# Four second-layer weight tiles loaded and prepared between the last expert's two units

## The chip, the core and the metric

The kernel runs on one core of one Trainium2 chip. The metric is the device time of one execution in microseconds (us). The core has a matrix engine (PE, with its weight loads shown apart as PEld), a vector engine (DVE), a scalar engine (ACT), GpSimd (POOL), and a queue (SP) that issues most of the transfers between the chip's memory and on-chip buffers. Each engine works through its own list of instructions in order and waits for the others by semaphores.

## What is computed

Three layers follow each other: attention, a mixture of eight experts in which each token goes to one, and a dense layer with a gate. Cut to what matters here:

```
def _moe_ref(x, w_gate, w_output_gate, w1, w2):      # x: 1536 x 512
    ...
    for e in range(E):                               # 8 experts
        mask = e_idx == e
        h = np.maximum(x[mask] @ w1[e], 0.0)         # 512 -> 1024
        ye = h @ w2[e]                               # 1024 -> 512
        out[mask] = gate_w[mask, None] * eom[mask, e, None] * ye

def _moe2_ref(x, w_in, w_out):                       # w_in: 512 x 2048
    h = x @ w_in
    g = h * (1.0 / (1.0 + np.exp(-h)))
    return (g @ w_out).astype(np.float32)            # w_out: 2048 x 512
```

The weights of the dense layer come as 64-bit floats.

## The kernel before

Each float32 matrix product is made of three matmuls: operands are split into a rounded high part and the rest as a low part, and high x high, high x low and low x high are summed.

**Experts.** `moe1` (L1042) runs ten units one after the other. A unit is some rows of one expert: two tiles of 128 rows, or one. The last two, here called unit A and unit B, are the first and the second 128 rows of expert 0. In `expert` (L965) such a one-tile unit first makes 2 x 12 matmuls `hr` (L986) in two groups. ACT copies each group to a buffer named `stage` (L989), PE transposes it (`htp`, L992), and `split` (L898) turns it into a high part (ACT, L899) and a low part (DVE, L904), both called `H`. Then 24 matmuls `yp` (L1022) make the output, DVE scales it into `ys` (L1027), and POOL scatters its rows to the table `x2` in memory (L824). Between unit A's two halves, the rows of unit B are transposed (`etp`) and split into `X`. Unit A's rows all belong to the first 768 tokens, so that the first block of the dense layer waits for unit A's scatter and not for unit B's.

**Dense layer.** `moe2` (L1218) has three blocks of 512 tokens. `load2` (L1204) reads a block's rows from `x2` (L834), transposes them (`tp`, L1213) and splits them into `XH` and `XL`; for the first block this stands in the middle of unit B. A block has 16 steps f. A step makes 12 matmuls `hp` (L1259), a sigmoid on ACT (L1265), a product on DVE (`sg`, L1266), a split into `GH` (ACT) and `GL` (DVE), and 12 matmuls `op` (L1238), which PE does one step late or more.

**Preparing a tile.** The dense layer has 16 weight tiles: four of `w_in` for f 0 to 7, four of `w_out` for f 0 to 7, and the same again for f 8 to 15, listed in that order by `weights2` (L1157). A tile is prepared in two halves of 512 columns. For each, SP loads 512 KB into a `stage` buffer (L1170); ACT scales the upper words (L1178) and copies the top bytes (L1181); DVE masks (L1182) and shifts (L1183) to put a 32-bit float together; ACT writes the high part of `w` (L899) and POOL the low part (L904):

```
nc.scalar.activation(gf, gf, AF.Copy, scale=float(2.0 ** (-112)))
nc.scalar.activation(l, by, AF.Copy, scale=1.0 / 32, bias=-31.0 / 64)
nc.vector.scalar_tensor_tensor(l, g, 2147483648, l, op0=ALU.bitwise_and, op1=ALU.bitwise_or)
nc.vector.scalar_tensor_tensor(g, g, 3, l, op0=ALU.logical_shift_left, op1=ALU.bitwise_or)
s.split(hi[:, sl], lo[:, sl], gf, s.nc.gpsimd)
```

There are seven `stage` buffers during the experts and four in the dense layer, used in turn; the one-tile units take one of the seven each for `hr`.

**Who orders the work.** The list `seq` in `moe1` holds the loads that are still to be made: 60 tiles of experts and then the 16 of the dense layer. Every unit takes up to four from it in its first half and up to four in its second, except those of expert 0, which take what the list `ta` says. Before, `ta` holds zeros: the eight earlier units take 60 expert tiles and 4 dense ones, and the 12 that are left are prepared in the first block of the dense layer, one at each of its steps f 0 to 11 (`w2.pop(0)()`). Inside a stage the order on each engine is fixed when the program is built.

Of the kernel before, what the change touches and what calls it, by code (L numbers as in the profile page):

```python
# [634 lines left out]
class Moe:  # L635
# [406 lines left out]
    def moe1(s, w2, free):  # L1042
        tc = s.tc
        nc = s.nc
        pos = 6
        L = 0
        N1 = 12
        N0 = 8
        units = [(e, 0, 2) for e in range(1, pos)] + [(E, 0, 1)] + [(e, 0, 2) for e in range(pos, E)] + [(L, 0, 1), (L, 1, 1)]
        order = [u[0] for u in units[:-1]]  # L1050
        W = {}
        X = {}
        s.ew = {e: s.expert_weights(e) for e in range(E)}

        def item(e, i):
            if e == E and i == 0:
                with tc.issue_after(s.lastld):
                    ev = nc.sync.value_load(s.Ei[0:1, 0:1], min_val=0, max_val=E - 1)
                s.ew[E] = s.expert_weights(ev)
            W.setdefault(e, [None] * 8)[i] = s.ew[e][i]()  # L1060

        def prep(u):
            e, h, n = u
            xt = s.rows('xt', s.xo, slice(0, 128), 1) if e == E else s.rows('xt', s.xst, slice(e * CAP + h * 128, e * CAP + (h + n) * 128), n, apart=u == units[0])
            x = s.lift(xt, n)
            X[u] = (s.labels(xt, n), x)
        s.hold = s.hold0
        for i in range(N0):
            if i == 4:
                s.hold = 2  # L1070
                with tc.issue_after(s.lastlow):
                    for _ in s.plan2:
                        pass
                s.lastlow = s.lastplan
            item(order[0], i)
        s.hold = False

        idle = s.ps_h.tile([128, 512], F32, tag='h', name='idle')
        with tc.issue_after(s.att.lastpe):
            for _ in range(33):  # L1080
                r = nc.tensor.matmul(idle, lhsT=s.ones, rhs=s.tri.unsqueeze(1).to_broadcast([128, 4, 128]), start=True, stop=True)
        with tc.issue_after(r.ins):
            prep(units[0])
        with tc.issue_after(s.lastlow):
            for f in s.lows:
                f()
        with tc.issue_after(s.lastrow), tc.issue_after(s.lastlow):
            for i in range(N0, 8):
                item(order[0], i)
            for i in range(N1 - 8):  # L1090
                item(order[1], i)
        s.gp = free()
        seq = [lambda e=e, i=i: item(e, i) for e in order for i in range(8)][N1:] + w2
        take = lambda n: [seq.pop(0) for _ in range(min(n, len(seq)))]
        x2 = []
        ta = [0, 0, 0, 0]
        for p, u in enumerate(units):
            e, h, n = u
            fx, x = X.pop(u)
            def first2():  # L1100
                x2.append(s.load2(0))

                idle = s.ps_h.tile([128, 512], F32, tag='h', name='idle2')
                with tc.issue_after(s.lasttp):
                    for _ in range(10):
                        nc.tensor.matmul(idle, lhsT=s.ones, rhs=s.tri.unsqueeze(1).to_broadcast([128, 4, 128]), start=True, stop=True)
            nxt = (lambda: prep(units[p + 1])) if p + 1 < len(units) else first2
            a, b = (4 if p else 16 - N1, 4) if e != L else ta[2 * h:2 * h + 2]
            s.expert(fx, x, n, W[e], take(a), nxt, take(b), first=p == 0)
        sig = s.fp.tile([128, 2, 4], F32, tag='f', name='sig')  # L1110
        with tc.high_priority(), tc.issue_after(s.lasth):
            nc.scalar.activation(sig[:, 0, 0:1], s.ident[:, 0:1], AF.Sigmoid)
        return (x2[0], seq)
# [218 lines left out]
```

## Time and profile before

| | us |
|---|---|
| median of three timed runs | 778.09 (777.33 to 779.23) |
| the profiled execution | 782.32 |
| its span, from the first to the last instruction | 780.2 |
| PE busy | 738.0 (95% of the span) |
| DVE busy | 485.6 (62%) |
| ACT busy | 436.6 (56%) |
| POOL busy | 322.7 (41%) |
| unit A's first matmul | at 456.5 |
| first block of the dense layer, first matmul | at 488.3 |

All places in time below are microseconds from the start of the span of the profiled execution. PE's busy time is that of pipelined matmuls whose ends overlap the next one's start: how many of them start in a stretch tells more of its pace than the busy share does. Busy time of the other engines counts an instruction from its start to its end, with what it waits for inside.

### The profile page before, as it was taken

How to read it: one execution, taken by the hardware profiler on the slowest of the kernel's cores; microseconds unless marked ns; L12 is line 12 of the kernel's file. 1: busy time of each engine (PE TensorE's matmuls, PEld its weight loads, DVE VectorE, ACT ScalarE, POOL GpSimd, SP SyncE). 2: the span in 40 equal slices, each digit the busy share in tenths (PEclk: the TensorE clock that was granted, in tenths of full speed). 3: DMA queues.
4: the chain of work that ended last, by engine and by line, in shares of the span. 5: the costliest groups of instructions: out<-in, count | busy, mean ns of one | idle time of the engine just before them, and what ended most of it. 6: DMA issues, size and time to landing. Idle time of an engine off the chain costs nothing.

```text
span 780.2 us, 14156 instructions
## 1 busy us (share of the span) xinstructions
PE 738.0 (95%) x5540; PEld 626.2 (80%) x5540; DVE 485.6 (62%) x823; ACT 436.6 (56%) x711; POOL 322.7 (41%) x259
## 2 busy tenths in 40 slices
PE   7889999999998799999999999989999999999995
PEld 6678998999998398888978877766787888878884
DVE  5769788877977666896568952899624222232222
ACT  5768889889875346655456653878423122131212
POOL 4677887878653376653334360455300000000000
PEclk9789999999999999999999999999999999999998
DMA  8769899998994578976557714666101000010001
GB/s 272 163 140 234 182 180 163 209 182 159 219 184 167 181 251 312 316 259 241 207 190 274 223 54 172 218 189 210 43 1 55 0 1 1 0 55 1 0 1 57
DMA packets 132984, 116.31 MB, mean 149 GB/s; under 512 B 97607, under 2 KB 103751, under 8 KB 132912
## 3 DMA queue, kind: packets, MB, share of 16 engines
q1 hardware_dynamic: 129632, 109.03, 52.3%
q0 software_dynamic: 3280, 6.33, 2.2%
q8 instruction: 45, 0.74, 0.4%
q14 instruction: 27, 0.22, 0.1%
HBM read 71.67 MB, written 18.45 MB: 116 GB/s over the span
## 4 chain that ended last, share of the span: by engine, by line
PE 61%; DVE 18%; issue 7%; ACT 6%; DMA 5%; POOL 2%; DVEq 0%; SPq 0%; ACTq 0%; POOLq 0%
PE op L1238 14%; PE hp L1259 13%; PE yp L1022 8%; PE hp L1006 6%; DVE m L423 4%; PE sp L402 3%; DMA stage<-in_moe_w_in 2%; PE sp L404 2%; PE hr L986 2%; DVE pt L460 2%; PE tp L190 2%; PE ptp L449 2%; ACT w L899 2%; PE cl L207 1%; POOL w L904 1%
## 5 line engine op out<-in xcount | busy, mean ns | idle before, releaser
L904 POOL TENSOR_TENSOR w<-stage,w 128x512 fp32r<-128x512 f32 (+1 forms) x54 | 105.1, 1953 | 98.8 <-ACT w L899 81.8
L1259 PE MATMUL hp<-XH,w 128*128 128x512 f32 (+1 forms) x392 | 124.0, 394 | 3.7 <-DVE sg L1266 3.5
L1238 PE MATMUL op<-w,GH 128*128 128x512 f32 x384 | 113.5, 396 | 0.1
L423 DVE TENSOR_REDUCE m<-sp 128x1 f32<-128x768 f32 x96 | 91.2, 951 | 34.4 <-PE sp L404 31.0
L469 POOL TENSOR_TENSOR p<-p,p 128x768 f16<-128x768 f32 x58 | 95.2, 1649 | 34.0 <-DVE p L468 18.5
L899 ACT ACTIVATE w<-stage 128x1024 fp32r<-128x1024 f32 (+1 forms) x104 | 94.7, 939 | 20.5 <-DVE stage L1183 8.2
L1266 DVE TENSOR_TENSOR sg<-hp,sg 128x512 f32<-128x512 f32 (+1 forms) x49 | 33.2, 678 | 111.8 <-ACT sg L1265 111.8
L425 ACT ACTIVATE p<-sp,m 128x768 f32<-128x768 f32 x96 | 86.1, 897 | 14.1 <-DVE m L423 13.9
L904 DVE TENSOR_TENSOR w<-stage,w 128x1024 fp32r<-128x1024 f32 x50 | 86.9, 1759 | 8.6 <-ACT w L899 8.5
L1265 ACT ACTIVATE sg<-hp 128x512 f32<-128x512 f32 (+1 forms) x49 | 28.8, 587 | 113.4 <-PE hp L1259 112.3
L1259 PEld LDWEIGHTS hp<-XH,w 128*128 128x128 f32 x392 | 73.2, 188 | 22.9 <-DVE sg L1266 5.4
L1006 PEld LDWEIGHTS hp<-X,w 128*128 128x128 f32 x672 | 84.8, 190 | 8.5 <-DVE HL L1008 4.0
L1006 PE MATMUL hp<-X,w 128*128 128x256 f32 x672 | 87.7, 284 | 4.1 <-DVE HL L1008 2.2
L1238 PEld LDWEIGHTS op<-w,GH 128*128 128x128 f32 x384 | 71.9, 188 | 17.7 <-ACT GH L899 1.0
L1259 PE MATMUL hp<-XL,w 128*128 128x512 f32 (+1 forms) x196 | 75.1, 391 | 0.0
L1238 PE MATMUL op<-w,GL 128*128 128x512 f32 x192 | 69.0, 399 | 3.5 <-DVE GL L904 3.3
L1022 PE MATMUL yp<-w,HH 128*128 128x512 f32 x224 | 68.9, 397 | 0.0
L402 PE MATMUL sp<-KA,QA 128*128 128x384 f32 x192 | 62.5, 407 | 2.9 <-ACT p L425 2.3
L493 PE MATMUL o<-vh,pt 128*128 128x66 f16 x576 | 62.0, 195 | 0.4 <-DVE pt L460 0.4
L494 PE MATMUL o<-vl,pt 128*128 128x64 f16 x576 | 61.5, 192 | 0.0
L495 PE MATMUL o<-vh,pt 128*128 128x66 f16 x576 | 61.1, 192 | 0.0
L493 PEld LDWEIGHTS <-pt 128*128 128x128 f16 x576 | 52.3, 96 | 7.2 <-issue 5.9
(221 smaller groups left out, 1454.7 us busy)
## 6 DMA issues: line engine op xcount, KB each, us to landing
stage<-in_moe_w SPq DMA_DIRECT2D x72, 512.0 KB, 4.8
stage<-in_moe_w_in SPq DMA_DIRECT2D x16, 512.0 KB, 4.3
stage<-in_moe_w_out SPq DMA_DIRECT2D x16, 512.0 KB, 4.5
xst<-z SPq DMA_DIRECT2D x8, 516.0 KB, 5.4
xt<-xst SPq DMA_DIRECT2D x6, 516.0 KB, 5.1
vt<-in_v SPq DMA_DIRECT2D x4, 768.0 KB, 6.6
xt<-x SPq DMA_DIRECT2D x6, 512.0 KB, 4.3
out_x<-os SPq DMA_DIRECT2D x12, 256.0 KB, 2.5
```

The source lines that it names most:

```text
L402: nc.tensor.matmul(sp[:, g, :384], lhsT=QA[:, t], rhs=KAf[:, g * 384:(g + 1) * 384], start=True, stop=False)
L423: st['min'] = nc.vector.tensor_reduce(m, sv, axis=AX.XY, op=ALU.min).ins
L425: st['exp'] = nc.scalar.activation(p32, sv, AF.Exp, bias=m, scale=-1.0).ins
L469: s.nc.gpsimd.tensor_sub(p16[:, 1], p32, p16[:, 0])
L493: nc.tensor.matmul(o[:, t, 0:D + 2], lhsT=pt[:, 0, kt], rhs=vh[:, kt], start=kt == 0, stop=False)
L494: nc.tensor.matmul(o[:, t, 0:D], lhsT=pt[:, 0, kt], rhs=vl[:, kt], start=False, stop=False)
L899: s.lasthi = s.nc.scalar.activation(hi, src, AF.Copy).ins
L904: f = lambda: (eng or s.nc.vector).tensor_sub(lo, src, hi).ins
L1006: nc.tensor.matmul(hp, lhsT=W1[k][w][:, f * 128:(f + 1) * 128], rhs=x[:, k, :N], start=n == 0, stop=n == 11)
L1022: nc.tensor.matmul(yp, lhsT=h[:, f, i * 128:(i + 1) * 128], rhs=w, start=n == 0, stop=n == 23)
L1238: nc.tensor.matmul(op[i], lhsT=g[:, i * 128:(i + 1) * 128], rhs=w, start=f == 0 and m == 0, stop=f == 15 and m == 2)
L1259: nc.tensor.matmul(h, lhsT=I[k, f // 8][w][:, fs], rhs=x[:, k, c], start=n == 0, stop=n == 11)
```

## The change

Two entries of the list become 2. Unit A therefore takes two dense-layer tiles from the list in its first half and two in its second: the four of `w_out` for f 0 to 7. The eight tiles that are left are prepared at the steps f 0 to 7 of the first block.

```diff
@@ -1093,7 +1093,7 @@
         seq = [lambda e=e, i=i: item(e, i) for e in order for i in range(8)][N1:] + w2
         take = lambda n: [seq.pop(0) for _ in range(min(n, len(seq)))]
         x2 = []
-        ta = [0, 0, 0, 0]
+        ta = [2, 2, 0, 0]
         for p, u in enumerate(units):
```

What this does to the engines' lists, at three places. The numbers behind names count buffers; the halves of the four tiles are `stage_7185`, `7193`, `7202`, `7210`, `7279`, `7287`, `7296` and `7304` in the changed kernel.

POOL, from the scatters of the unit ahead of unit A to that of unit B. The scatter of unit A is the one of `ys_7244` before and `ys_7312` now, that of unit B the next one. Before:

```order
L904 TENSOR_TENSOR w_7139<-stage_7148,w_7139 128x512
L824 DMA x2_72<-ys_7092,f_6733 1536x512
L824 DMA x2_72<-ys_7156,f_6733 1536x512
L824 DMA x2_72<-ys_7244,f_6969 1536x512
L824 DMA x2_72<-ys_7363,f_7215 1536x512
```

and now:

```order
L824 DMA x2_72<-ys_7092,f_6733 1536x512
L824 DMA x2_72<-ys_7156,f_6733 1536x512
L904 TENSOR_TENSOR w_7184<-stage_7185,w_7184 128x512
L904 TENSOR_TENSOR w_7184<-stage_7193,w_7184 128x512
L904 TENSOR_TENSOR w_7201<-stage_7202,w_7201 128x512
L904 TENSOR_TENSOR w_7201<-stage_7210,w_7201 128x512
L824 DMA x2_72<-ys_7312,f_6969 1536x512
L904 TENSOR_TENSOR w_7278<-stage_7279,w_7278 128x512
L904 TENSOR_TENSOR w_7278<-stage_7287,w_7278 128x512
L904 TENSOR_TENSOR w_7295<-stage_7296,w_7295 128x512
L904 TENSOR_TENSOR w_7295<-stage_7304,w_7295 128x512
L824 DMA x2_72<-ys_7431,f_7249 1536x512
```

Four subtractions now stand ahead of unit A's scatter, and four more ahead of unit B's.

ACT, from the split of unit B's rows (`X`) to the split of its hidden rows (`H`). Before:

```order
L899 ACTIVATE X_7207<-etp_7208 128x4x128
L989 ACTIVATE stage_7249<-hr_7251 128x512
L989 ACTIVATE stage_7249<-hr_7272 128x512
L899 ACTIVATE H_7250<-htp_7265 128x512
L899 ACTIVATE H_7250<-htp_7286 128x512
```

and now the end of the same piece, from the scaling of the seventh half:

```order
L1178 ACTIVATE stage_7296<-stage_7296 128x512
L1181 ACTIVATE stage_7296<-stage_7296 128x512
L899 ACTIVATE w_7278<-stage_7279 128x512
L1178 ACTIVATE stage_7304<-stage_7304 128x512
L1181 ACTIVATE stage_7304<-stage_7304 128x512
L899 ACTIVATE w_7278<-stage_7287 128x512
L989 ACTIVATE stage_7317<-hr_7319 128x512
L899 ACTIVATE w_7295<-stage_7296 128x512
L989 ACTIVATE stage_7317<-hr_7340 128x512
L899 ACTIVATE w_7295<-stage_7304 128x512
L899 ACTIVATE H_7318<-htp_7333 128x512
L899 ACTIVATE H_7318<-htp_7354 128x512
```

Unit B's two `H` copies now stand behind the high part of the eighth half, which waits for DVE's shift of it. In unit A, likewise, the scaling and byte copy of the second half now stand between the copy of `hr` and the two `H` copies; DVE's mask of that half stands ahead of its first `H`, and its masks and shifts of the last four halves stand ahead of unit B's `H`. On SP the eight loads stand ahead of the two reads of the first block's rows (`xt`), where none stood.

DVE, in the first block of the dense layer, from the step f 7 on. Before, to f 8:

```order
L1266 TENSOR_TENSOR sg_7725<-hp2_7724,sg_7725 128x512
L1182 SCALAR_TENSOR_TENSOR stage_7893<-stage_7893 128x512
L1183 SCALAR_TENSOR_TENSOR stage_7893<-stage_7893 128x512
L904 TENSOR_TENSOR GL_7727<-sg_7725,GH_7726 128x512
L1182 SCALAR_TENSOR_TENSOR stage_7934<-stage_7934 128x512
L1183 SCALAR_TENSOR_TENSOR stage_7934<-stage_7934 128x512
L1182 SCALAR_TENSOR_TENSOR stage_7942<-stage_7942 128x512
L1183 SCALAR_TENSOR_TENSOR stage_7942<-stage_7942 128x512
L1266 TENSOR_TENSOR sg_7774<-hp2_7773,sg_7774 128x512
```

and now, to f 9:

```order
L1266 TENSOR_TENSOR sg_7793<-hp2_7792,sg_7793 128x512
L904 TENSOR_TENSOR GL_7795<-sg_7793,GH_7794 128x512
L1266 TENSOR_TENSOR sg_7842<-hp2_7841,sg_7842 128x512
L904 TENSOR_TENSOR GL_7844<-sg_7842,GH_7843 128x512
L1266 TENSOR_TENSOR sg_7908<-hp2_7907,sg_7908 128x512
```

The masks and shifts that stood here are gone; the last of the eight tiles' shifts now stands ahead of f 6.

## Rows read from the trace of the kernel before

**Rows 1.** Stretches: length, then busy us (instructions) of PE, PEld, DVE, ACT, POOL, granted clock, DMA share, GB/s.

```profile
456.00:488.00 32.00, 31.39 (x151) 23.91 (x149) 11.30 (x16) 12.91 (x24) 11.87 (x10) 1.00 0.33 125
488.30:510.00 21.70, 21.69 (x97) 17.64 (x98) 18.43 (x24) 16.94 (x31) 10.46 (x7) 1.00 0.67 208
510.00:534.00 24.00, 20.46 (x87) 15.24 (x87) 23.03 (x25) 19.19 (x34) 13.27 (x10) 1.00 0.62 186
534.00:558.00 24.00, 21.68 (x89) 15.21 (x89) 22.21 (x25) 18.46 (x32) 13.67 (x9) 1.00 0.47 152
```

**Rows 2.** Waits of PE from 380 on: total us, times, longest.

```profile
PE hp L1259 <- DVE sg L1266: 3.5, 5, 1.4
PE op L1238 <- DVE GL L904: 3.3, 4, 1.6
```

**Rows 3.** The chain that ended last, a step behind the first block's preparation: start, us.

```profile
571.91 2.80 PE hp L1259 x12
```

**Rows 4.** Groups by line, 534 to 558: count, busy us, mean ns, idle before.

```profile
L1213 PE MATMUL tp<-ident,xt 128*128 128x128 f32 x8 | 1.2, 272 | 0.0
```

**Rows 5.** Order of time, DVE: start, us; the shift of the eighth tile's second half.

```profile
531.49 1.71 DVE L1183 SCALAR_TENSOR_TENSOR stage<-stage 128x512 uint32<-128x512 uint32 x1
```

**Rows 6.** Order of time, DVE's shift and POOL's subtraction, beside each other and alone.

```profile
455.85 1.32 POOL L904 TENSOR_TENSOR w<-stage,w 128x512 fp32r<-128x512 f32 x1 [3.93 <-issue]
455.96 1.76 DVE L1183 SCALAR_TENSOR_TENSOR stage<-stage 128x512 uint32<-128x512 uint32 x1
...
457.13 1.77 POOL L904 TENSOR_TENSOR w<-stage,w 128x512 fp32r<-128x512 f32 x1
...
499.87 0.69 DVE L1183 SCALAR_TENSOR_TENSOR stage<-stage 128x512 uint32<-128x512 uint32 x1
```

**Rows 7.** Groups by line, DVE, 488 to 558.

```profile
L1183 DVE SCALAR_TENSOR_TENSOR stage<-stage 128x512 uint32<-128x512 uint32 x24 | 31.4, 1312 | 0.6
```

**Rows 8.** Order of time, POOL, around unit A.

```profile
455.85 8.11 POOL L904 TENSOR_TENSOR w<-stage,w 128x512 fp32r<-128x512 f32 x6 [3.93 <-issue]
464.12 0.99 POOL L824 DMA_INDIRECT x<-ys,f  x1 [0.16 <-issue]
...
472.40 0.97 POOL L824 DMA_INDIRECT x<-ys,f  x1 [6.00 <-DVE ys L1027]
```

**Rows 9.** Order of time, SP: the dense layer's loads and the reads behind them.

```profile
430.10 20.47 SPq L1170 DMA_DIRECT2D stage<-in_moe_w_in  x8
475.09 0.89 SPq L834 DMA_DIRECT2D xt<-x  x2
```

**Rows 10.** Issues at 450.2 and at 475.1: KB, us from issue to landing.

```profile
stage<-in_moe_w_in SPq DMA_DIRECT2D x1, 512.0 KB, 3.6
...
xt<-x SPq DMA_DIRECT2D x1, 512.0 KB, 3.7
```

**Rows 11.** Order of time, ACT, in units A and B.

```profile
463.68 0.60 ACT L989 ACTIVATE stage<-hr 128x512 f32<-128x512 f32 x1 [3.55 <-PE hr L986]
464.17 0.59 ACT L899 ACTIVATE H<-htp 128x512 fp32r<-128x512 f32 x1
...
477.47 0.59 ACT L899 ACTIVATE H<-htp 128x512 fp32r<-128x512 f32 x1
```

**Rows 12.** Order of time, DVE, in units A and B.

```profile
471.37 0.75 DVE L1027 TENSOR_SCALAR ys<-yp,f 128x512 f32<-128x512 f32 x1 [3.81 <-PE yp L1022]
478.09 0.69 DVE L904 TENSOR_TENSOR H<-htp,H 128x512 fp32r<-128x512 f32 x1 [5.97 <-ACT H L899]
```

**Rows 13.** Order of time, PE, in units A and B.

```profile
465.95 5.38 PE L1022 MATMUL yp<-w,H 128*128 128x512 f32 x22
...
478.94 0.63 PE L1213 MATMUL tp<-ident,xt 128*128 128x128 f32 x4
```

**Rows 14.** PE at the experts' start: a wait, then two stretches (columns of rows 1).

```profile
271.46 0.66 PE L961 MATMUL etp<-ident,xt 128*128 128x128 f32 x4 [2.51 <-DMA xt<-xst]
...
269.60:273.00 3.40, 1.31 (x8) 0.84 (x8) 3.40 (x13) 0.63 (x2) 0.00 (x0) 1.00 0.97 276
273.10:276.50 3.40, 2.88 (x13) 2.88 (x14) 2.80 (x13) 0.67 (x2) 1.97 (x2) 0.50 0.98 335
```

## Prediction

> **What bounds the kernel now.** I read the stretches first, then PE's waits, then the engines' lists in order of time around units A and B. In the experts' last two units, 456 to 488, PE is busy 31.4 of 32.0 us while DVE, ACT and POOL stand idle for more than half of it [rows 1]. A reader should see two things there: the other engines have room, and PE has none, so that whatever makes PE wait here is paid in full. In the first block of the dense layer it is the other way round: from 510 to 558 DVE is busy 45.2 of 48.0 us and PE waits, for `sg` 3.5 us and for `GL` 3.3 us in all, nearly all of it here [rows 1, 2].
>
> The loss there is larger than those waits, so I take it from counts. Undisturbed, twelve matmuls start in 2.80 us, 0.233 us each [rows 3]. From 534 to 558 PE starts 89, eight of them transposes that take 1.2 us [rows 1, 4]: 81 x 0.233 + 1.2 = 20.1, so 3.9 of the 24 us are lost. From 510 to 534 it starts 87; with as many transposes, 79 x 0.233 + 1.2 = 19.6, 4.4 lost. From 488 to 510, with 97 instructions in 21.7 us, nothing is lost. The first block thus pays about 8.3 us for preparing twelve tiles.
>
> **What the change gives back.** The eighth tile's last shift ends at 533.2 [rows 5]. The four tiles that leave the block are those behind it, so what is lost from 534 on goes: **3.9 us**. Its lower end is 3.2, if the transposes are priced as matmuls (24 - 89 x 0.233), or if the eighth tile's last steps still hold PE for a moment; its upper end is 4.4, half of the loss plus the like of the first stretch. The eight earlier tiles keep their place against the block's steps, so their 4.4 us stay. What is removed from the block (8 loads, 16 ACT steps and 8 copies, 16 DVE steps, 8 on POOL) is added to units A and B; nothing disappears.
>
> **What it costs, first stop: unit A.** I call the eight halves h1 to h8. Each needs one of seven buffers, freed by POOL's subtractions of the tiles before: six in 8.11 us from 455.85, 1.35 each [rows 8], so that h1 to h6 can be issued from 457.2 to 464.0, one behind the other. A load lands after 3.6 us [rows 10]: h1 at 460.8, h2 at 462.5, h3 at 463.6. They are in time. But ACT now scales h2 and copies its bytes between the copy of `hr` that ends at 464.28 and the first `H`, which began at 464.17 [rows 11]: two steps of about 0.6 us. `H` starts at 465.4, DVE's mask of h2 comes next, then `H`'s low part, and the 22 `yp` that began at 465.95 [rows 13] begin at about 467.4. This is **1.4 us**, all on PE. It hides behind nothing, since PE's list has no other work there.
>
> **Second stop: unit B, by the port.** The shift took 1.76 us while POOL's subtraction ran from 455.85 to 457.17, and 0.69 alone; the next subtraction, behind that shift, took 1.77 instead of 1.3 [rows 6]. Over the block the shifts average 1.31 [rows 7]. So a mask or shift and a subtraction exclude each other, and when both wait they take turns. Each half then needs about 0.6 (mask) + 0.6 (shift) + 1.3 (subtraction) = 2.5 us of one resource, as long as the subtractions follow closely. Eight halves are 20 us; the first mask can start at 462.2, behind h1's two ACT steps. I followed the lists from there with these durations. DVE: shift of h2 ends at 467.3, of h3 at 469.7, of h4 at 472.1, of h5 at 474.4 (behind h3's subtraction), `ys` of unit A at 475.1 (before: 472.1 [rows 12]), shift of h6 at 476.9, of h7 at 479.3 (behind h5's subtraction), mask of h8 at 481.1, shift of h8 at 482.9. ACT's high part of h8 ends at 483.6, and only then come unit B's `H` (before 477.47 [rows 11]), their low parts, and the transposes of the first block. h8's buffer is that of h1, free at 468.5; it lands at 472, so its load holds nobody.
>
> The low part of the first `H` ends at 484.85, where it ended at 478.78 [rows 12]; the transposes `tp` that began at 478.94 [rows 13] begin at 484.9. That is **5.9 us** for both stops together, the 1.4 contained. The later blocks' reads and the block's own first loads shift with it and are waited for no longer than before.
>
> **Third path, POOL's scatter and SP.** Unit A's scatter stood alone at 472.40; the read of its rows was issued at 475.09, 2.69 later, and landed after 3.7 us, at 478.8 [rows 8, 9, 10], which is just when the transposes began. So this path has no slack. Now four subtractions stand ahead of the scatter; the fourth, h4's, whose high part leaves ACT at 473.9 and which then takes its turn behind the shift of h5, ends at 475.75; the scatter starts at 475.9, the read at 478.6 (behind eight loads on SP, the last issued at 468.6), and it lands at 482.3. Alone this would cost 3.4 us; beside the 5.9 it is covered. If the port costs nothing, this is what is left, so the stop lies between 3.4 and about 7.0 us (one more subtraction, 1.3, in front of h8's shift). I take 5.9, nearest to what rows 6 show.
>
> **The clock.** Between PE's last `hr` and `yp` of unit B, at 478.8 to 484.2, PE would have only four transposes to do in between. The trace has a like place: at the experts' start PE waited 2.51 us, in a stretch of 3.4 us with 1.31 busy, and the next 3.4 us went at a granted clock of 0.50, the lower level of 1.2 GHz; before, it was 1.00 [rows 14]. At half clock 3.4 us do the work of 1.7. Part of it may fall into the wait: between 0.7 and 1.7, I take **1.2 us**.
>
> The Trainium skill says of this (page "TensorE: Matmul & The Clock Gate", section on the HAM clock gate) that the throttled state is the default and that activity releases it. By that rule the spell comes here; without it the sum is the second rival's. Of the port, the skill's "SBUF — State Buffer" (section "SBUF: two separate sides") states a rule against this change: the pair shared by DVE and GpSimd is an exclusive lock, and the loser "fully blocks". Rows 6 agree with it; without it the sum is the third case's.
>
> **Sum.** 5.9 + 1.2 - 3.9 = +3.2 us. The profiled execution took 782.32 with a span of 780.2, of which these terms are parts; I put the difference on the median of the timed runs, 778.09: **781.3**.
>
> **Cases.**
> 1. Forecast, as above: 781.3, chance 0.42. Its terms range over 3.4 to 7.0, 0.7 to 1.7 and 3.2 to 4.4; a tenth of this case, at the low ends, stays within 0.3%.
> 2. The same stop without the half clock: 5.9 - 3.9 = +2.0, 780.1. For it: PE does do transposes within the wait, and elsewhere waits of 1.4 us left the clock at 1.00 [rows 1, 2]. Against: this wait is twice as long as that of rows 14. Chance 0.17.
> 3. Subtractions fall between the shifts without collisions, and the scatter's path alone decides: 3.4 - 3.9 = -0.5, 777.6. For it: in the block 24 shifts take 31.4 us [rows 7], which is 14 at about 1.75 and 10 at 0.69, so that four in ten meet no subtraction. Against: here the halves lie ready in a row, and ACT's list, not a transfer, sets their distance. With two collisions fewer ahead of the scatter (0.45 each, 1.77 against 1.32 [rows 6]) the stop would be 2.5 and the gain at most 4.4: 776.2 is the low end. Chance 0.21.
> 4. The other side: the low parts keep ahead of the scatter. If POOL has done the first four subtractions by 473.8, because h1 to h4 are prepared wholly inside the 22 `yp`, then `ys`, scatter and read keep their place behind PE, the preparation hides in idle DVE and ACT [rows 1], and only the first stop is paid: 1.4 - 3.9 = -2.5, 775.6, faster. It decides when the fourth subtraction ends no later than the scatter is ready to go, 472.4 + 1.4; I find it 2 us late. Chance 0.14.
> 5. Worse: one more subtraction gets in front, the half clock falls wholly behind the wait and the gain is at its lower end: 7.0 + 1.7 - 3.2 = +5.5, 783.6. Chance 0.06.
>
> That the change does not do what it says is no case here: the lists show the halves moved.
>
> **How the numbers follow.** About 0.3%, 2.3 us, is what a measurement of this kernel can tell from no change. Slower: nine tenths of case 1 and case 5, 0.44. Same: the rest of case 1, cases 2 and 3, 0.42. Faster: case 4, 0.14. Cases 1, 2 and 3 hold 0.80, so the range covers them with the spread of case 1's terms, from 776.2 to 783.0 (7.0 + 1.2 - 3.2 = +5.0). As cases of both signs are in it, case 1's own range is 779.6 (4.3 + 1.1 - 3.9, the stop halfway to 3.4) to 783.0.
>
> **What would show it.** Right: unit B's `H` on ACT stands behind a wait for the shift of h8; `tp` of the first block begins about 6 us later than unit A's first matmul would put it; the first block's `hp` begins near 494 and the block's steps reach full pace some 24 us earlier against its start; the granted clock falls to 0.5 once between 482 and 492. Case 3 would show `tp` waiting for the read of `x2`, 3 to 4 us late; case 4 would show neither wait. The prediction is wrong in its gain if PE still waits for `sg` or `GL` behind the eighth tile, or if the block's full pace comes no earlier.

## The result, and the profile after

The changed kernel is slower. Its median is 784.34 us in six timed runs (782.49 to 785.84), against 778.0 in six of the kernel before on the same chip: a ratio of 1.0079, with a 95% interval of 1.0061 to 1.0097, that is 4.7 to 7.5 us more. On a second chip the ratio was 1.0048 (1.0024 to 1.0072), 1.9 to 5.6 us more. The median of the changed kernel was nearly the same there, 785.59, but that of the kernel before was 781.65; on the three further chips of this study it was 781.56 to 781.63, so the 778.0 of the first chip is the lowest of five. The forecast was slower by 3.2 us, at 781.3 with a range to 783.0; the direction was right, and the time lies 1.3 us above the range.

For finding where the time went I measure each trace from unit A's first matmul, because the lists of all engines are the same in both kernels up to there, and yet that matmul starts anywhere from 454.0 to 462.2 us in the 14 executions of this study. Three stretches follow: A to the first transpose `tp` of the first block, `tp` to the block's first `hp`, and that `hp` to the start of the last `op`. Two executions of each kernel, in us:

| | A to `tp` | `tp` to `hp` | `hp` to last `op` | A to last `op` |
|---|---|---|---|---|
| before | 22.47 | 9.37 | 283.64 | 315.48 |
| before, again | 22.52 | 9.39 | 283.73 | 315.63 |
| after | 28.77 | 11.35 | 280.01 | 320.13 |
| after, again | 28.75 | 10.80 | 281.36 | 320.92 |

So the change costs 6.3 us up to `tp` (5.9 forecast), 1.4 to 2.0 up to `hp` (1.2 forecast), and gives back 2.4 to 3.6 behind it (3.9 forecast): +4.65 and +5.3 in all.

PE's waits from 450 to 600 in the changed kernel (total us, times, longest), which answer [rows 2]:

```profile
PE htp L992 <- ACT stage L989: 4.2, 3, 3.4
PE hp L1259 <- DVE sg L1266: 2.5, 2, 2.2
PE yp L1022 <- ACT H L899: 1.2, 2, 1.0
PE op L1238 <- DVE GL L904: 0.4, 1, 0.4
```

The first and the third wait are new, and they are the two stops. PE in order of time (start, us; in brackets the idle time ahead and what ended it), answering [rows 13]:

```profile
464.29 0.74 PE L1022 MATMUL yp<-w,H 128*128 128x512 f32 x2 [0.96 <-ACT H L899]
...
465.62 5.38 PE L1022 MATMUL yp<-w,H 128*128 128x512 f32 x22
...
481.25 1.11 PE L992 MATMUL htp<-ident,stage 128*128 128x128 f32 x4 [3.36 <-ACT stage L989]
482.57 1.22 PE L1022 MATMUL yp<-w,H 128*128 128x512 f32 x2 [0.21 <-ACT H L899]
483.59 1.05 PE L1213 MATMUL tp<-ident,xt 128*128 128x128 f32 x4
```

Against the first `hr` (454.83 here, 456.47 before) the 22 `yp` are 1.31 us later than before, which is the first stop. The second is the wait of 3.36 at 481.25. The chain behind it is read on three engines, first ACT, in unit B [rows 11]:

```profile
476.59 0.59 ACT L989 ACTIVATE stage<-hr 128x512 f32<-128x512 f32 x1
480.02 0.68 ACT L899 ACTIVATE w<-stage 128x512 fp32r<-128x512 f32 x1 [2.85 <-DVE stage L1183]
480.60 0.60 ACT L989 ACTIVATE stage<-hr 128x512 f32<-128x512 f32 x1
481.35 0.68 ACT L899 ACTIVATE w<-stage 128x512 fp32r<-128x512 f32 x1 [0.16 <-DVE stage L1183]
481.94 1.07 ACT L899 ACTIVATE H<-htp 128x512 fp32r<-128x512 f32 x2
```

The second copy of `hr` (480.60) stands behind the high part of h7, which waited 2.85 us for DVE's shift. DVE at the same time [rows 6, 12]:

```profile
472.31 1.70 DVE L1183 SCALAR_TENSOR_TENSOR stage<-stage 128x512 uint32<-128x512 uint32 x1
473.92 0.74 DVE L1027 TENSOR_SCALAR ys<-yp,f 128x512 f32<-128x512 f32 x1
474.58 0.68 DVE L1182 SCALAR_TENSOR_TENSOR stage<-stage 128x512 uint32<-128x512 uint32 x1
475.30 0.69 DVE L1183 SCALAR_TENSOR_TENSOR stage<-stage 128x512 uint32<-128x512 uint32 x1
475.91 3.36 DVE L1182 SCALAR_TENSOR_TENSOR stage<-stage 128x512 uint32<-128x512 uint32 x1
479.30 0.69 DVE L1183 SCALAR_TENSOR_TENSOR stage<-stage 128x512 uint32<-128x512 uint32 x1
...
482.55 1.29 DVE L904 TENSOR_TENSOR H<-htp,H 128x512 fp32r<-128x512 f32 x2 [1.23 <-ACT H L899]
```

and POOL [rows 8], then SP's read of the rows [rows 9]:

```profile
472.01 1.44 POOL L904 TENSOR_TENSOR w<-stage,w 128x512 fp32r<-128x512 f32 x1 [0.29 <-ACT w L899]
474.94 1.19 POOL L824 DMA_INDIRECT x<-ys,f  x1 [1.49 <-ACT w L899]
476.15 2.55 POOL L904 TENSOR_TENSOR w<-stage,w 128x512 fp32r<-128x512 f32 x2
```

```profile
477.85 0.89 SPq L834 DMA_DIRECT2D xt<-x  x2
```

The mask of h7 takes 3.36 us: it stands still under two subtractions in a row, which end at 478.70. `hr` copy, transposes, `H` and `tp` follow from its end.

Stretches (length; busy us and instructions of PE, PEld, DVE, ACT, POOL; granted clock, DMA share, GB/s), answering [rows 1, 14]: units A and B, then three stretches of the first block, then three around the stop.

```profile
454.30:486.30 32.00, 26.40 (x112) 20.14 (x112) 25.27 (x27) 23.65 (x42) 23.49 (x17) 0.92 0.66 226
495.00:517.00 22.00, 22.00 (x99) 17.85 (x100) 19.39 (x24) 16.36 (x31) 9.76 (x7) 1.00 0.59 198
517.00:541.00 24.00, 21.32 (x87) 16.31 (x86) 21.63 (x24) 18.39 (x32) 13.95 (x10) 0.93 0.52 169
541.00:565.00 24.00, 23.64 (x105) 18.70 (x104) 7.43 (x11) 6.06 (x11) 1.03 (x1) 1.00 0.01 1
479.00:481.00 2.00, 0.00 (x0) 0.00 (x0) 1.93 (x4) 0.97 (x2) 0.22 (x1) 1.00 0.82 286
481.10:487.90 6.80, 6.44 (x19) 4.93 (x20) 2.20 (x4) 3.83 (x7) 2.64 (x2) 0.50 0.93 313
487.90:494.90 7.00, 6.89 (x37) 4.72 (x35) 3.11 (x5) 3.26 (x7) 0.99 (x1) 1.00 0.21 85
```

In 32 us from unit A on, PE starts 112 instructions where it started 151. From 541, 46 us behind the block's first `hp`, it starts 105 in 24 us, the full pace of [rows 3]; before, that pace came some 70 us behind it. But from 517 to 541 it still starts only 87, as many as before [rows 1]. The granted clock is 0.50, the lower level of 1.2 GHz, for 6.8 us from 481.1, behind 2 us in which PE did nothing. In this execution a second such spell stands at 522 (3.4 us at 0.51 from 522.15), behind a wait of 2.2 us for `sg`; the second execution of the same kernel has a wait of 2.4 us there and no spell.

### The profile page after: what moved, and what is told of

Same layout as the page of the kernel before. It is cut to its first block, busy times and chain, and to the rows that moved or that the text cites. A ratio compares the mean times of both kernels' runs of the same rounds, so it can differ in the third digit from the quotient of the medians.

```text
span 782.7 us, 14162 instructions
## 1 busy us (share of the span) xinstructions
PE 738.1 (94%) x5540; PEld 627.5 (80%) x5540; DVE 487.0 (62%) x823; ACT 435.6 (56%) x711; POOL 321.5 (41%) x259
## 4 chain that ended last, share of the span: by engine, by line
PE 62%; DVE 17%; ACT 7%; issue 7%; DMA 4%; POOL 1%; SPq 0%; DVEq 0%; ACTq 0%; POOLq 0%
PE op L1238 15%; PE hp L1259 14%; PE yp L1022 7%; PE hp L1006 6%; DVE m L423 4%; PE sp L402 3%; PE sp L404 2%; DVE pt L460 2%; PE ptp L449 2%; DMA stage<-in_moe_w_in 2%; PE tp L190 2%; ACT w L899 2%; PE o L493 2%; PE hr L986 1%; DVE w L904 1%
## 5 line engine op out<-in xcount | busy, mean ns | idle before, releaser
L1238 PEld LDWEIGHTS op<-w,GH 128*128 128x128 f32 x384 | 72.8, 190 | 17.3
```

The costliest lines, as they stand in the source:

```text
L1238: nc.tensor.matmul(op[i], lhsT=g[:, i * 128:(i + 1) * 128], rhs=w, start=f == 0 and m == 0, stop=f == 15 and m == 2)
```

## Experiments

**The same two kernels on another chip.** No edit.

> The unchanged kernel, for a second trace. Theory: the profiled execution of before (782.3 us, span 780.2) was some 4 us slower than the six timed ones (777.3 to 779.2), and ahead of unit A, where it spent 13.7 us in one spell of half clock at 30.8; a second trace then has a span near 776 with unit A's first matmul near 452, and the 315.5 us from there to the last op matmul unchanged. Rival: the second trace looks like the first (span about 780, unit A at 456), and the timed runs are short for a reason that no trace shows.

> The changed kernel, for a second trace. Theory: as in the first, unit A's first matmul to the first transposes of the dense layer takes 28.8 us (before 22.5), a half clock spell of 3.4 or 6.8 us follows it, and the block loses 5.3 us at most; ratio to before 1.006 to 1.010. Rival: the 6.3 us were one draw, and this execution is 2 to 3 us off.

Ratio of the first 1.0002 (0.9981 to 1.0023), of the second 1.0048 (1.0024 to 1.0072). The second trace of the kernel before has a span of 785.6 and unit A at 461.7, which is neither the theory (776 and 452) nor the rival (780 and 456); only the 315.5 us from there on came out (315.63). The stretches are in the table above: from one execution to the other they repeat to 0.1 us up to `tp`; up to `hp` they differ by 0.02 (before) and 0.55 (after), and behind `hp` by 0.1 (before) and 1.4 (after). What follows is judged by these stretches first, and by the timed ratio where there is one.

**The moved tiles' low parts on DVE instead of POOL.**

```diff
-                    s.split(hi[:, sl], lo[:, sl], gf, s.nc.gpsimd)
+                    s.split(hi[:, sl], lo[:, sl], gf, s.nc.vector if s.moved else s.nc.gpsimd)
...                                  # s.moved is set for the four moved tiles
```

> The changed kernel, but the low parts of the four moved tiles are made on DVE and not on POOL. Theory (the port): masks and shifts of units A and B no longer wait for subtractions, the 3.4 us mask of the seventh half and the 1.7 us shifts go to 0.69; DVE has 8 x (0.6 + 0.6 + 0.7) = 15 us instead of 20, the scatter stands alone on POOL, and the stall falls from 6.3 to about 3, with at most one half clock spell: 3 to 5 us faster than the changed kernel, 779 to 781. Rival (the order of ACT's list alone): ACT has as many steps ahead of unit B's H as before and DVE eight more; no faster than the changed kernel, 783 to 786.

Ratio 1.0071 (1.0047 to 1.0096); A to `tp` 30.22, `tp` to `hp` 10.84. The forecast, 3 to 5 us faster than the changed kernel, missed: as the rival said, it is no faster, though for another reason than ACT's list. In units A and B, masks and shifts behind POOL's last old subtraction now take about 0.7, and PE's wait at `htp` is down to 0.5. But unit A's scatter, DVE's last shift, and PE's wait for the rows that the scatter writes, read (POOL and DVE in order of time; PE's waits):

```profile
477.65 6.59 POOL L824 DMA_INDIRECT x<-ys,f  x1 [7.20 <-DVE ys L1027]
...
482.70 0.69 DVE L1183 SCALAR_TENSOR_TENSOR stage<-stage 128x512 uint32<-128x512 uint32 x1
```

```profile
PE tp L1215 <- DMA xt<-x: 6.5, 1, 6.5
```

The scatter took 6.59 us where it took 0.97 [rows 8]. DVE ran masks, shifts and subtractions, one behind the other, until 483.39 and then `H`, which reads one operand from PE's result memory; the scatter ended 0.85 behind the 483.39. So the long masks and shifts of the second stop are shown to come from POOL's subtractions: without them PE's waits at `htp` fall from 4.2 to 0.5 us, although ACT has the same steps to do. The collision has a second side, which this edit brought out: steady work of DVE holds up a scatter on POOL. The Trainium skill describes a trap of this kind (page "SBUF — State Buffer", section "SBUF: two separate sides"): while DVE runs an operation in a two-port performance mode, GpSimd is locked out of the ports that the two share and cannot write the descriptors of a transfer. The trap names that mode; the row here shows such a hold beside masks, shifts and subtractions with two operands in the on-chip memory, and no run shows in which mode they ran.

**The gain by itself.** Two kernels in which four tiles are neither loaded nor prepared, so that part of the result is left out. In the first it is the four moved ones. In the second it is the four of `w_in` for f 8 to 15, which stand in unit A's places instead, so that the eight tiles left in the block are all of `w_out`.

```diff
-                    O[f // 2] = ld((lambda hf: wout...
+                    O[f // 2] = I[f // 2, 0] if f < 8 else ld((lambda hf: wout...
...                                  # the second kernel has this instead:
-                    I[k, h] = ld((lambda hf: win...
+                    I[k, h] = I[k, 0] if h else ld((lambda hf: win...
...
-        X, w2 = m.moe1(m.weights2(), free)
+        t = m.weights2()
+        X, w2 = m.moe1(t[:4] + t[8:12] + t[4:8] + t[12:], free)
```

> The changed kernel without the four moved tiles: they are not loaded or prepared, and the dense layer uses the first four w_in tiles in their place (part of the result is left out by this). It gives the gain alone. Theory: units A and B run as before, without stall or half clock, and the first block loses 3.8 to 5.3 us instead of 9.1: 3.8 to 5.3 us below before, 772.7 to 774.2. Rival (the gain is smaller, because the block's start or its port sets its pace whatever stands behind): 775 to 778.

> As no_prep (four tiles are neither loaded nor prepared, part of the result is left out), but the eight tiles that the block prepares are all w_out tiles, in the first four places the same ones as before the change. Theory (the block's gain fell short because w_in tiles stand at its third and fourth place, whose loads land about 2 us later there than w_out's): the wait for the seventh half's load is gone, the block loses 4.5 to 5.2 us instead of 6.6, and first hp to last op takes 279.1 to 279.9 us (no_prep 281.2, before 283.7). Rival (the pace is set by who stands in the block, not by which weights): 281 again.

Neither kernel has the costs: A to `tp` is 22.83 and 22.91, 0.4 above before, and `tp` to `hp` 9.38 in both, as before. But A to the last `op` falls by only 2.1 us in the first (313.44; ratio 0.9977, 0.9947 to 1.0006) and by 5.0 in the second (310.52; one time, 776.89). First `hp` to last `op` is 281.24 and 278.22; the first forecast (a gain of 3.8 to 5.3) missed, the second (279.1 to 279.9) fell short of the gain. So the gain of four tiles depends on what the other eight are, by 3.0 us.

**The clock by itself.** Twelve idle matmuls for PE between unit B's two transposes of `hr`.

```diff
+                if c and warm:              # warm is 12 for unit B
...
+                    with s.tc.issue_after(s.lasthtp):
+                        for _ in range(warm):
+                            nc.tensor.matmul(idle, lhsT=s.ones, rhs=..., start=True, stop=True)
```

> The changed kernel with twelve idle matmuls (2.6 us at full clock) between unit B's two groups of hidden-row transposes, where PE waited 3.4 us. Counted from unit A's first matmul to the first transposes of the dense layer, from these to its first hp, and on to its last op. Theory (the half clock of 6.8 us behind the stall is due to PE's idling): the stall stays (28.8 us to the transposes, at most 0.5 more), the spell at about 480 is gone, and the second stretch takes 9.4 us instead of 10.8 to 11.4. Rival (the spell is chance, as those in the attention part): it is still there, 10.8 or more.

The stop stays (A to `tp` 28.59), and the half clock is gone (same stretch as above, 481.1 to 487.9):

```profile
481.10:487.90 6.80, 6.13 (x32) 4.65 (x31) 2.40 (x4) 4.11 (x7) 2.27 (x2) 1.00 0.83 280
```

`tp` to `hp` is 8.90, 1.9 and 2.5 below the two executions without them; `hp` to last `op` stays at 281.34. Against the 9.4 of the kernel before, the spell cost 1.4 to 2.0 us. This is one execution; with a wait of 3.4 us for `hr` and no idle matmuls the spell stands in three of three (the two of the changed kernel and the one with another order of tiles, below). One time, 783.21; A to the last `op` 318.82.

**Two tiles instead of four**, in unit A's first half only; in the second kernel with their low parts on DVE as above.

```diff
-        ta = [2, 2, 0, 0]
+        ta = [2, 0, 0, 0]
```

> Only two of the four tiles move, in unit A's first half; ten stay in the block. Theory (the stall grows with the halves that stand ahead of unit B's H and of the scatter): four halves cost the first stop, 1.4 us, and the scatter behind four subtractions about 1 more; 23.9 to 25.0 us from unit A to the transposes (before 22.5, changed 28.8), no half clock of more than 3.4 us, and the block gains 0.7 to 2.2: 315 to 316.5 in all (before 315.5, changed 320.1 and 320.9). Rival (any subtraction ahead of the scatter brings the whole chain): 27 or more to the transposes.

> As two_first, with the low parts of the two moved tiles on DVE. Theory: POOL's list is as before the change, DVE's port work (8 masks and shifts, 4 low parts, 8 us) is over before unit A's scatter is due, so that neither the lock nor a starved scatter holds PE: 23.5 to 24.2 us to the transposes, 9.4 on to hp, 0.7 to 2.2 gained in the block: 314.5 to 315.9 in all, the same as before or at most 1 us faster. Rival (the scatter is starved here too, as with all four tiles on DVE): 26 or more to the transposes.

A to `tp` 25.04 and 24.30, `tp` to `hp` 9.38 and 9.37 with no half clock there, `hp` to last `op` 282.88 and 283.38. The first gave one time, 784.37, and A to last `op` 317.30; the second a ratio of 1.0013 (0.9987 to 1.0040) and 317.04. Both sums miss their forecasts (315 to 316.5 and 314.5 to 315.9). The first stop stays: unit B's first `hr` starts 16.0 us behind unit A's in both, as in the changed kernel, where it was 14.7 before. The second shrinks to a wait of `tp` for the rows, 1.36 and 0.62 us, and a PE wait that short leaves the clock at 1.00. But two tiles fewer give only 0.3 to 0.8 us behind `hp`. Here, too, `w_in` has moved up, to the third place in the block, which the next experiment is about; and in the second kernel a half-clock spell stands behind `hp`, between 518 and 522.

**The order of the eight tiles.** All four tiles moved as in the change; of the eight left, the `w_out` ones come first, as in the kernel before.

```diff
-        X, w2 = m.moe1(m.weights2(), free)
+        t = m.weights2()
+        X, w2 = m.moe1(t[:8] + t[12:] + t[8:12], free)
```

> The changed kernel, with the eight tiles of the first block in another order: the four of w_out for f 8 to 15 first, then the four of w_in for f 8 to 15, so that the eight places have the sources that they had before the change (w_out, then w_in). Theory, the order of the sources: the gain fell short of 3.9 because w_in, whose loads are strided, now stands first, lands up to 8.0 us after its issue and holds ACT at the sixth and seventh half. Then from the block's first hp to the last op it takes 277.0 to 278.6 us (280.0 and 281.4 in the changed kernel, 283.6 before), and from unit A's first matmul to the last op 317.0 to 318.6 (320.1 and 320.9; before 315.5); ratio to the kernel before about 1.003 to 1.005. Rival, the stall's aftermath: the early steps lose more because the block begins with the stall and the half clock behind it, whatever is loaded. Then both stay within 0.7 of the changed kernel's, 280 to 281.4 and 320 to 321. The stall itself stays at 28.8 from unit A to the first tp in both.

A to `tp` 28.79, `tp` to `hp` 10.69, `hp` to last `op` 278.62, A to last `op` 318.11; ratio to the kernel before 1.0027 (1.0000 to 1.0053). The lists of ACT, DVE, POOL and PE are the same as in the changed kernel up to buffer numbers, so only the data that the loads fetch differ, and the stretch behind `hp` is 1.4 and 2.7 us shorter. The place is ACT's scaling of the sixth and seventh half. The changed kernel:

```profile
507.51 0.68 ACT L1178 ACTIVATE stage<-stage 128x512 f32<-128x512 f32 x1 [1.62 <-DMA stage<-in_moe_w_in]
...
511.32 0.68 ACT L1178 ACTIVATE stage<-stage 128x512 f32<-128x512 f32 x1 [1.54 <-DMA stage<-in_moe_w_in]
```

with `w_out` first:

```profile
505.08 0.69 ACT L1178 ACTIVATE stage<-stage 128x512 f32<-128x512 f32 x1 [0.62 <-DMA stage<-in_moe_w_out]
...
507.85 0.67 ACT L1178 ACTIVATE stage<-stage 128x512 f32<-128x512 f32 x1 [0.45 <-DMA stage<-in_moe_w_out]
```

In the kernel before, with `w_out` in these places too, ACT's two waits are 1.98 and 0.39. The loads behind the seventh and eighth half, from issue to landing (KB, us), in the changed kernel and then in the kernel before, the first of each pair issued 1.3 us behind a read of rows:

```profile
stage<-in_moe_w_in SPq DMA_DIRECT2D x1, 512.0 KB, 8.0
stage<-in_moe_w_in SPq DMA_DIRECT2D x1, 512.0 KB, 7.5
```

```profile
stage<-in_moe_w_out SPq DMA_DIRECT2D x1, 512.0 KB, 6.4
stage<-in_moe_w_out SPq DMA_DIRECT2D x1, 512.0 KB, 7.1
```

ACT waits in its list for these halves, and the sigmoids and `GH` behind them come late: PE's longest wait for `sg`, 2.2 us, is the second row of the first view above, and with `w_out` first the longest is 0.4. All of PE's waits for `sg`, `GL` and `GH` in the first 75 us of the block come to 2.9 us and a half-clock spell in the changed kernel's first execution, to 5.2 in its second, and to 2.6 with `w_out` first. The wait of 2.2 to 2.5 us for `sg`, 26 to 27 us behind the first `hp`, stands in all seven traces with `w_in` in the third place of the block, and in none of the others (1.9 at most there); it was followed by a half-clock spell in three of the seven and by none in four. That a `w_in` load reads its rows with gaps between them, and a `w_out` load without, is in the code; whether this is why it lands later was not tried.

**Without the two stops.** Tiles are prepared behind unit A's last `H` on ACT, with the subtractions held until its scatter is issued. Two tiles; three tiles; and three tiles where the third one's masks wait until the scatter has landed, and the subtractions until that tile's last shift is done. The tiles left come in the order of the kernel before.

```diff
-        ta = [2, 2, 0, 0]
+        ta = [0, 2, 0, 0]            # 3 in the second kernel
...
+                with tc.issue_after(s.last):      # unit A's scatter
+                    for f in s.later:             # the held subtractions
+                        f()
...
-                    for x in s.x2low:
+                    for x in [s.lasth] if s.later is not None else s.x2low:
```

> Two tiles of w_out moved instead of four (the list is 0, 2, 0, 0), their preparation on ACT and DVE held until unit A's last H copy has been issued, and their four subtractions on POOL held until unit A's scatter has been issued; the ten tiles left in the block come w_out (four), w_in (four), w_out (two), as the first ten places had them before. If the two stops are what I say they are (ACT and DVE steps ahead of H, and the port shared by DVE's masks and shifts with POOL's subtractions, ahead of the scatter), both are gone: unit A's first matmul to the first tp 22.4 to 23.2 us (22.5 before, 28.8 in the changed kernel), tp to hp 9.4, no half clock there; the scatter about 1 us long. The block then loses some 6.4 us where before it lost 9.1 (two tiles fewer): first hp to last op 280.6 to 281.6, unit A's first matmul to the last op 312.5 to 313.8 against 315.5, ratio 0.996 to 0.998. Rival: the gain comes from four tiles or not at all, since the steps f 8 and f 9 alone still lose what the last ones lost: first hp to last op 283 or more, ratio 1.000 within 0.002.

> As late2, with three tiles moved (0, 3, 0, 0) and nine left in the block (w_out four, w_in four, w_out one). Now five masks and shifts on DVE stand behind unit A's ys, beside the scatter and the held subtractions. By the port theory they and the subtractions exclude each other again: shifts of 1.7 us or more, unit B's H low part 1.5 to 4 us late, the scatter longer than 1 us, unit A's first matmul to the first tp 24 to 27; the block gains about 4 (first hp to last op 279.3 to 280.3); unit A's first matmul to the last op 313 to 316.5, ratio 0.997 to 1.002. Without the port the stall stays under 1 us and the sum is 311.5 to 312.5, ratio 0.994 to 0.996.

> As late3 (three tiles moved, nine left), but the third tile's masks and shifts on DVE wait until unit A's scatter has landed, and the held subtractions on POOL wait until the last of these shifts is done, so that DVE and POOL do not meet, neither at the scatter nor at the subtractions. If DVE's masks and shifts are what stretched late3's scatter to 3.6 us, the scatter is back at 1.0 to 1.2 us, the wait of the first tp for the rows falls from 3.4 to about 1, masks and shifts take 0.69 each, and from unit A's first matmul to the first tp it is 23.0 to 24.5 us (25.8 in late3) with tp to hp at 9.4 and no half clock; first hp to last op near late3's 278.2 (278 to 280), unit A's first matmul to the last op 310.5 to 312.8 against 315.5 before; ratio to the kernel before 0.991 to 0.996. Rival: the scatter is long because more work is ready for POOL and the rows' read queues behind more transfers, not because of DVE. Then the first tp still waits 3 us or more, and the sum stays at 314 to 315.5.

| | A to `tp` | `tp` to `hp` | `hp` to last `op` | A to last `op` | ratio to before |
|---|---|---|---|---|---|
| two tiles | 23.47 | 9.39 | 281.98 | 314.83 | 0.9962 (0.9937 to 0.9986) |
| three tiles | 25.80 | 10.93 | 278.17 | 314.90 | 1.0020 (0.9993 to 1.0048) |
| three, DVE gated | 23.53 | 9.40 | 281.61 | 314.54 | 1.0001 (0.9974 to 1.0028) |

Unit A's scatter on POOL in the three kernels, in the second with the end of DVE's work beside it:

```profile
473.07 1.17 POOL L824 DMA_INDIRECT x<-ys,f  x1 [6.92 <-DVE ys L1027]
```

```profile
478.87 3.58 POOL L824 DMA_INDIRECT x<-ys,f  x1 [6.78 <-DVE ys L1027]
...
480.31 1.29 DVE L1191 SCALAR_TENSOR_TENSOR stage<-stage 128x512 uint32<-128x512 uint32 x2
```

```profile
472.61 1.18 POOL L824 DMA_INDIRECT x<-ys,f  x1 [6.81 <-DVE ys L1027]
```

With two tiles one shift is left behind unit A's `ys`, and the scatter takes 1.17 us. With three, five masks and shifts follow without a pause until 481.60, and the scatter ends 0.85 behind that, as it did above. When DVE is made to wait, it takes 1.18, `tp` comes 2.3 us earlier and no longer waits for the rows: the rival, a queue of transfers, falls. POOL did nothing else in any of the three at this place, so it is DVE's masks and shifts that hold the scatter. In the middle kernel I had forecast shifts of 1.7 us and a late `H` as well; neither came, since the subtractions began only when the shifts were done. The price was the scatter alone: PE waits 3.4 us for the rows, and a spell at half clock follows.

The gated kernel gives its gain back further on. Its subtractions end at 486, the buffers come free late, and the block's own first four loads are issued at 484.78, 28.8 us behind unit A's first matmul, where it was 476.09, 19.6 behind, before. ACT then waits for the first half of the block:

```profile
484.78 1.95 SPq L1182 DMA_DIRECT2D stage<-in_moe_w_out  x4
```

```profile
488.43 0.66 ACT L1190 ACTIVATE stage<-stage 128x512 f32<-128x512 f32 x1 [1.15 <-DMA stage<-in_moe_w_out]
```

That this wait is the whole difference of 3.4 us behind `hp` to the middle kernel is argued, not shown; the order of the block's steps differs as well.

By the stretches the three lie within 0.4 us of each other, 0.6 to 0.9 below the 315.5 of before. By the timed ratio only the kernel with two tiles is faster than the kernel before: 779.15 us median against 781.63 on that chip. The stretches show 0.7 of these 2.5 us; where the rest comes from is open. Of the three sums only the middle kernel's is as forecast; the gated one misses by 1.7 us. The kernel with two tiles misses by 1.0, and of that 0.4 lie behind `hp` and 0.3 up to `tp`: `ys` stands behind a mask on DVE, the scatter comes 0.7 later against unit A's start than before, and PE waits 1.1 us for the rows.

## Why the prediction was right and where it was not

**The stop: right in size, with one wrong step inside.** 6.3 us measured, 5.9 forecast. The first stop is 1.31 for 1.4. At the second, the step "when both wait they take turns" failed: h7's mask was passed over by a second subtraction and took 3.36, where one collision would have taken about 1.8. ACT waited for the shift of h7 and not of h8, and what stood behind it was unit B's second copy of `hr`, one step ahead of the `H` that the prediction named. Fewer collisions elsewhere made up for it (h6's mask and shift took 0.68 and 0.69). The third path stood as forecast, covered: the scatter at 474.94 is 4.2 us later against unit A's start than before (3.5 forecast), and PE did not wait for the rows. Its cause is another one, though: the fourth subtraction had ended at 473.45, and what was late was `ys`, behind DVE's shift of h5 (1.70 us), ending at 474.66. (The row of the scatter names ACT's high part, which ended 0.04 later and which the scatter does not need.) Case 3, that path alone, did not come; nor did case 4, in which the subtractions had to be done 17.3 us behind unit A's start and were done after 18.6.

**The clock: right, slightly short.** One spell behind the wait, where it was forecast, twice as long as the one of [rows 14]: 2.0 and 1.4 us in the two executions for 1.2, the first above the range of 0.7 to 1.7. The second rival, no spell, falls; the kernel with idle matmuls, in one execution, shows both that PE's idling brought the spell and the price.

**The gain: the step that failed.** "The eight earlier tiles keep their place against the block's steps, so their 4.4 us stay." They keep their places, but they are other tiles: with `w_out` for f 0 to 7 gone, `w_in` moves to the front, lands later there, and holds ACT. The block gained 3.6 and 2.4 us for 3.9, the second below the range of 3.2 to 4.4; with the sources in the old order it gains 5.0 (283.64 less 278.62), above the upper end. The loss per place was read from the traces as if it belonged to the place; part of it belongs to the source of the tile. One reading beside it was loose as well: of the 3.5 us for `sg` in [rows 2], 1.3 lie behind the first block, so 5.5 of the 6.8 us of these waits fall into it and not nearly all.

**The sum.** With the measured terms, 6.3 + 2.0 - 3.6 = +4.7 and 6.3 + 1.4 - 2.4 = +5.3, nearest to the fifth case (+5.5), which I gave 0.06, though that one counted on a longer stop (7.0) than came. Put on the 778.09 that the forecast started from, this is 782.7 and 783.4, at the upper end of the range (783.0); each of the three terms was off to the slow side, the gain in the second execution most, by 1.5. The difference of the medians on the first chip, 6.3, lies 1.0 to 1.6 above the traces, and that of the second chip, 3.7, lies 1.0 to 1.6 below. So the way from the traces to 784.34 is not explained by the change's terms. The traces show nothing of the change in the part ahead of unit A, whose length varies by several us between executions of one kernel; I take this as scatter, and what causes it stays open.

## To carry to other kernels

When work is moved out of a stage, ask what moves up into its place: the items left are not the same items, and their loads may land later where they now stand. Work of DVE that reads two operands from the on-chip memory, next to subtractions or a scatter on POOL, behaved here as one resource and not two: watch which path (the waiting DVE step or the scatter) carries the end. To put them into separate stretches of time freed the scatter here (1.18 us for 3.58), but the timed ratio did not fall; the buffers came free later, and that this is the reason is argued only. Two tiles placed behind the critical steps (314.8 us from unit A on, before 315.5) did better than four placed among them (320.1 and 320.9).

## What the hardware did that I had not expected

POOL and DVE do not always alternate. A mask that waited under a subtraction was passed over by the next one and took 3.36 us (again 3.36 in the second execution), where one collision costs 1.7 to 1.8 and none 0.69. The trace of the kernel before has such a step too, ahead of unit A: a mask that began under a scatter and was held by the subtraction of twice the width behind it.

```profile
437.93 1.25 POOL L824 DMA_INDIRECT x<-ys,f  x1 [0.30 <-ACT stage L1181]
438.58 3.58 DVE L1182 SCALAR_TENSOR_TENSOR stage<-stage 128x512 uint32<-128x512 uint32 x1
439.19 2.43 POOL L904 TENSOR_TENSOR w<-stage,w 128x1024 fp32r<-128x1024 f32 x1
```

A scatter issued from POOL can stand still for as long as DVE runs masks and shifts without a pause: 3.58 and 6.59 us for 0.97. It needs a pause behind such a step: it finished 0.85 us behind the last one in both, and also in the two kernels with 1.17 and 1.18, where one shift was left (ending at 473.39 and 472.94); in the changed kernel the gap between a mask and a shift, from 475.26 to 475.30, was enough, and it finished 0.87 behind the mask. Why the pause matters, no run here shows.
